# Retention plus MLP on one core: batches 0 and 1 loaded two positions a partition, with 64x64 matmul tiles and a new order of the first stage

## The chip, the core and the metric

The kernel runs on one core of a Trainium2 chip, as one launch. The metric is the device time of one execution in microseconds (us), the median of several runs; lower is better. Besides this, one execution is profiled. Names of engines are those of the profile: PE (matmuls; PEld its weight loads), DVE, ACT and POOL (elementwise work), SP (which issues nearly all DMAs). Each engine works through its own queue in program order.

## The reference

Eight batches of eight heads, 576 positions, head size 64, float32. Attention is without softmax, with a decay for each head; its output goes through a two-layer MLP with a swish whose slope is given for each hidden unit.

```python
def _attn_ref(q, k, v):
    B, H, S, D_ = q.shape                        # 8, 8, 576, 64
    scores = 1.0 / np.sqrt(D_) * np.matmul(q, k.transpose(0, 1, 3, 2))
    gamma = 1.0 - 2.0 ** (-5.0 - np.arange(H, dtype=np.float32))
    rel = np.arange(S)[:, None] - np.arange(S)[None, :]
    Dmat = np.where(rel >= 0, gamma[:, None, None] ** rel[None, :, :], 0.0)
    return np.matmul(scores * Dmat[None], v).astype(np.float32)

def _moe_ref(x, w_in, w_out, beta):              # 4608x512, 512x2048, 2048x512, 2048
    h = x @ w_in
    g = h * (1.0 / (1.0 + np.exp(-beta * h)))
    return (g @ w_out).astype(np.float32)

x = attn_out.transpose(0, 2, 1, 3).reshape(B * S, H * D)     # then _moe_ref
```

## The kernel before

**Attention in chunks.** The decay is split into factors of the query and of the key position: q is multiplied by `gq`, v by `gv`, and the scores get a mask of zeros and ones only. The first 512 positions of a batch are four chunks of 128 (c = 0 to 3); the last 64 positions of all batches are done together at the end. For a chunk the kernel computes scores (keys on the partitions, `a_sc`), masks them with `causal` into `R` (DVE), and adds two matmuls up in one output `O`: values times `R` (`a_O`), and, for c > 0, the state of the earlier chunks times q (`a_cross`). The state is the running sum of keys times values (`a_st`, PSUM tile `st`), copied to `sbds[c]` in bfloat16. `a_x` copies `O` into `xT`, the MLP's input.

**Layouts of batches 0 and 1.** q is loaded with four positions on a partition (`load_q`, 1 KB runs), half of the heads at a time. k and v of a chunk are loaded with one position on a partition (`load_kv`, 256-byte runs, 256 KB each). `pre_q` scales q (DVE), `pre` casts k to `kn` and scales v to `vn` (POOL), `t_q` and `t_k` turn q and k on PE into a PSUM tile `T`, which ACT or DVE copies to `qT` and `kT`. Scores use 64x128 tiles of PE (two heads in the two halves of the rows), outputs 128x64, states and cross terms 128x128. Batches 2 and on have another layout, 64x64 tiles, and turn q and k by DMA; the change leaves them as they are.

**Loads.** SP issues, in this order: q of batch 0 in two halves; k and v of chunks 0 and 1, k of chunks 2 and 3, v of chunks 2 and 3; w_in in eleven pieces; then, in the merged part, w_out, q and k and v of batch 1, q of batch 2, and so on.

**The first stage** (lines 869 to 915) is written out by hand, in program order; `warm_up(n)` are float32 matmuls on zeros between the real ones. Their PSUM tile has the tag `mm`, of which there are three buffers; `O` and `sc` have two each, `st` one.

**The merged part.** `fill` is the list of PE's dense steps (up- and down-projections of the blocks), with `d0` the step of the first down-projection and `u1` the step of the second block's first up-projection. `streams` are lists of (step, function); `merged` puts each function into program order ahead of the step with that number. Batch 1's attention steps and the loads and preparation of the later batches are such streams. From block 3 on, the down-projection is done with seven products in place of eight (`seven_mm`, `seven_a`, `seven_b`).

Of the kernel before, what the change touches and what calls it, by code (L numbers as in the profile page):

```python
# [19 lines left out]
def kernel(  # L20
# [54 lines left out]
    q_tiles, kv_tiles = {}, {}  # L75
# [13 lines left out]
    def load_kv(n, js=(0, 1)):  # L89
# [7 lines left out]
        for j in js:  # L97
            src = (k, v)[j][b].rearrange("h s d -> s h d")
            if b < QB:
                nc.sync.dma_start(t[:, j], src[c * P:(c + 1) * P])  # L100
            elif c % 2 == 0:
                nc.sync.dma_start(t[:, j], src[c * P + TL:(c + 1) * P + TL])
            else:
                for x, at in enumerate(((c - 1) * P, (c + 1) * P - TL)):
                    nc.sync.dma_start(t[x * TL:(x + 1) * TL, j], src[at:at + TL])


    ahead = [(0, 0), (0, 1), (1, 0), (1, 1), (2, 0), (3, 0), (2, 1), (3, 1)]
    keys_first = [(0, 0), (1, 0), (0, 1), (1, 1), (2, 0), (3, 0), (2, 1), (3, 1)]
# [12 lines left out]
    load_q(0)  # L122
    for n, j in ahead:
        load_kv(n, (j,))
# [9 lines left out]
    for j, (step, mul) in enumerate(((1, CB), (P, 1))):  # L134
        nc.gpsimd.iota(pos[:, j, :CB], pattern=[[step, CB]], base=0, channel_multiplier=mul,
# [10 lines left out]
    for h in range(H):  # L146
# [12 lines left out]
    causal = consts.tile([P, P], BF16, name="causal")  # L159
    nc.gpsimd.memset(causal[:], 1.0)  # L160
    nc.gpsimd.affine_select(out=causal[:], in_=causal[:], pattern=[[1, CB], [CB, PC]], compare_op=ALU.is_ge,
                            fill=0.0, base=0, channel_multiplier=-1)
# [38 lines left out]
    def cast_w_in(g, kos=None):  # L201
        t = wts[g]
        f0, fn, rows = pieces[g]
        for ko in kos or range(rows[0].start, rows[-1].stop):
            if ko % 2 == 0:
                nc.gpsimd.tensor_copy(w_in_sb[:, ko, f0:f0 + fn], t[:, ko])  # L206
                continue
            nc.vector.tensor_copy(w_in_sb[:, ko, f0:f0 + fn], t[:, ko])
# [56 lines left out]
    def betas():  # L265
        pb = psum.tile([P, FO], F32, name="pb", tag="mm", bufs=3)
        nc.tensor.transpose(pb[:], beta_rows[:], ident_f[:FO, :FO])
        nc.scalar.copy(beta_sb[:], pb[:])
# [24 lines left out]
    def row_of(b, c):  # L293
        return CB + 1 + c % 2 * 2 + c // 2 if b >= QB else c
# [15 lines left out]
    def pre_q(b, n):  # L310
# [4 lines left out]
        if b < 2:  # L315
            hs, cs = slice(n // 2 * HP, (n // 2 + 1) * HP), slice(n % 2 * 2, n % 2 * 2 + 2)
            e = nc.vector
# [12 lines left out]
    def pre(i, js=(0, 1)):  # L330

        b, c = seq[i]
        if 0 not in js:
            v, g = kv_tiles.pop(i)[:, 1], gains(gv, row_of(b, c))
            if b < QB:
                nc.gpsimd.tensor_tensor(live[i]["vn"][:], v, g, ALU.mult)
            else:
                by_halves(live[i]["vn"], v, g)
# [24 lines left out]
        for to, hs in turned if b >= QB else [(slice(0, H), slice(0, H))]:  # L363
            nc.gpsimd.tensor_copy(kn[:, c % 2, to], t[:, 0, hs])  # L364
        if 1 in js:
            pre(i, (1,))

# [16 lines left out]
    def t_q(b, u):  # L384
        T = psum.tile([P, CB, 2, P], BF16, name="T", tag="mm" if u else "O", bufs=3 if u else 2)
        for i in range(CB):
            for p in range(2):
                nc.tensor.transpose(T[:, i, p, :], heads(batch[b]["qs"][:, i], 2 * u + p), ident[:])
        (nc.vector.tensor_copy if u else nc.scalar.copy)(batch[b]["qT"][:, :, 2 * u:2 * u + 2], T[:])

    def t_k(i):
        T = psum.tile([P, HP, P], BF16, name="T", tag="sc" if i in (CB + 2, CB + 3) else "O", bufs=2)
        for p in range(HP):
            nc.tensor.transpose(T[:, p, :], heads(live[i]["kn"], p), ident[:])
        (nc.vector.tensor_copy if i in (CB + 2, CB + 3) else nc.scalar.copy)(live[i]["kT"], T[:])

# [6 lines left out]
    def a_sc(i):  # L403
        L = live[i]
        L["R"] = R = sb.tile([P, 2, HP, P], BF16, name="R", tag="R", bufs=3)

        tag = "mm" if i == CB - 1 else "O" if i >= E and (i - E) % 2 else "sc"
        sc = [psum.tile([P, HP, P], F32, name="sc", tag=tag, bufs=3 if tag == "mm" else 2) for _ in range(2)]
        for p in range(HP):
            for j in range(2):  # L410
                r = slice(j * D, (j + 1) * D)
                rhs, view = q_cols(i, r, p)
                nc.tensor.matmul(view(sc[j][:, p, :]), L["kT"][r, p, :], rhs, start=True, stop=True,  # L413
                                 skip_group_check=True)
        m_b = causal[:].unsqueeze(1).to_broadcast([P, HP, P])
# [3 lines left out]
    def split(i):  # L419
        return i in (CB - 1, CB + 1)  # L420

    def new_O(i):
        b, c = seq[i]
        if split(i):
            tags = ("sc", "sc") if i == CB - 1 else ("O", "sc")
            live[i]["O"] = [psum.tile([P, 2, P], F32, name="O", tag=t, bufs=2) for t in tags]
# [22 lines left out]
    def a_O(i):  # L449

        b, c = seq[i]
        L = live[i]

        early = i < E
        if not early:
            new_O(i)
        R, vn = L["R"], L["vn"]
        crossed = c > 0
        for j, p in [(n % 2, n // 2) for n in range(H)]:
            nc.tensor.matmul(O_of(i, p)[j * D:(j + 1) * D], vn[:, 2 * p + j, :], R[:, j, p, :],  # L460
                             start=opens(i, p) and not (early and crossed), stop=early or not crossed,
                             skip_group_check=True)

    def a_x(i):
# [3 lines left out]
        if split(i):  # L468
            nc.vector.tensor_copy(x[:, :2], view(Os[0]))
            nc.scalar.copy(x[:, 2:], view(Os[1]))  # L470
# [3 lines left out]
    def a_st(i):  # L474

        b, c = seq[i]
        L = live[i]
        if c == 0:
            state_ps[b] = psum.tile([P, HP, P], F32, name="st", tag="st", bufs=1)
        st = state_ps[b]  # L480
        for p in range(HP):
            nc.tensor.matmul(st[:, p, :], heads(L["kn"], p), heads(L["vn"], p),
                             start=(c == 0 and p == 0), stop=True, skip_group_check=True)
        for j in range(2):
            r, cols = slice(j * D, (j + 1) * D), slice(j * D, (j + 1) * D)
            e = nc.vector.tensor_copy if i in (CB + 2, CB + 3) else nc.scalar.copy
            if c < CB - 1:
                e(sbds[c][r, :, cols], st[r, :, cols])
                continue
            e(ends[b][r, :2], st[r, :2, cols])  # L490
            e(ends[b][(1 - j) * D:(2 - j) * D, 2:], st[r, 2:, cols])
# [377 lines left out]
    warm_up(5)  # L869
    betas()  # L870
    betas_safe()
    for n in range(4):
        pre_q(0, n)
    t_q(0, 0)
    warm_up(1, 128)
    t_q(0, 1)
    pre(0)
    t_k(0)
    warm_up(2, 128)
    a_sc(0)  # L880
    a_st(0)
    pre(1)
    t_k(1)
    warm_up(1, 128)
    a_cross(0, True)
    a_O(0)
    a_x(0)
    a_sc(1)
    a_cross(1, True)
    pre(2, (0,))  # L890
    t_k(2)
    a_st(1)
    a_O(1)
    pre(3, (0,))
    a_sc(2)
    t_k(3)
    a_x(1)
    warm_up(1, 128)
    a_sc(3)
    a_cross(2, True)  # L900
    pre(2, (1,))
    a_st(2)
    a_O(2)
    a_x(2)
    pre(3, (1,))
    warm_up(2, 128)
    a_cross(3, True)
    a_O(3)
    cast_w_in(0, (0, 1))
    a_x(3)  # L910
    cast_w_in(0, (2, 3))
    a_st(3)
# [38 lines left out]
    def second(i):  # L951
        for f in (a_O, lambda j: a_cross(j, False), a_x):
            f(i)
            f(i + 1)
        a_st(i + 1)
# [5 lines left out]
               [(10.3, F(load_q, 1))] + [(10.3, F(load_kv, CB + n, (j,))) for n, j in keys_first],  # L961
# [5 lines left out]
               [(d0 + 8, F(pre, 4, (0,))), (d0 + 8, F(pre, 5, (0,))), (d0 + 9, F(pre, 4, (1,))), (d0 + 9, F(pre, 5, (1,))),  # L967
# [139 lines left out]
```

## Time and profile before

| what | value |
|---|---|
| median of the runs | 293.27 us (three runs, 292.98 to 293.93) |
| the profiled execution | 292.41 us |
| its span, from the first to the last instruction | 290.7 us |
| mean granted clock of PE | 0.999 |
| busy in the span | PE 281.9 (97%), PEld 175.7, DVE 186.1, ACT 171.5, POOL 139.1 us |
| first up-projection matmul (L819) | 18.44 us |
| DMA, 0 to 14.5 us | 216 GB/s |
| DMA, 18.4 to 40 us | 378 GB/s |

PE's matmuls are pipelined, so that its busy share is not a share of its peak; a hole in its row is read from the starts of its matmuls. "Idle before" names the engine or DMA whose work the profile infers to have ended a wait.

### The profile page before, as it was taken

How to read it: one execution, taken by the hardware profiler on the slowest of the kernel's cores; microseconds unless marked ns; L12 is line 12 of the kernel's file. 1: busy time of each engine (PE TensorE's matmuls, PEld its weight loads, DVE VectorE, ACT ScalarE, POOL GpSimd, SP SyncE). 2: the span in 40 equal slices, each digit the busy share in tenths (PEclk: the TensorE clock that was granted, in tenths of full speed). 3: DMA queues.
4: the chain of work that ended last, by engine and by line, in shares of the span. 5: the costliest groups of instructions: out<-in, count | busy, mean ns of one | idle time of the engine just before them, and what ended most of it. 6: DMA issues, size and time to landing. Idle time of an engine off the chain costs nothing.

```text
span 290.7 us, 8297 instructions
## 1 busy us (share of the span) xinstructions
PE 281.9 (97%) x3433; PEld 175.7 (60%) x3433; DVE 186.1 (64%) x340; ACT 171.5 (59%) x301; POOL 139.1 (48%) x259
## 2 busy tenths in 40 slices
PE   8799999999999998999999999999999999999995
PEld 6554446864544554448854885578547845784584
DVE  6563555804896396279889875995597555642673
ACT  5677546686878872765158625772576156837730
POOL 4766207872499397089759539625088100000000
PEclk9999999999999999999999999999999999999999
DMA  8999999996989999988999989990779430003004
GB/s 213 218 342 386 387 283 233 240 190 123 247 180 246 253 187 201 267 225 214 183 249 265 195 231 260 189 156 2 215 176 142 92 144 3 2 28 119 0 4 143
DMA packets 128886, 54.03 MB, mean 186 GB/s; under 512 B 110400, under 2 KB 121680, under 8 KB 128848
## 3 DMA queue, kind: packets, MB, share of 16 engines
q1 hardware_dynamic: 128816, 53.49, 77.9%
q8 instruction: 27, 0.44, 0.7%
q14 instruction: 11, 0.09, 0.1%
q10 hardware_dynamic: 32, 0.01, 0.0%
HBM read 36.71 MB, written 9.44 MB: 159 GB/s over the span
## 4 chain that ended last, share of the span: by engine, by line
PE 55%; DVE 5%; POOL 4%; DMA 2%; issue 1%; ACT 0%; SPq 0%; DVEq 0%
PE ph L727 27%; PE U L764 10%; PE Z L764 7%; PE W L764 6%; DMA qn<-in_q_dram 2%; DVE sa L748 2%; PE O L509 2%; PE po L837 2%; POOL vn L305 2%; POOL kn L364 1%; PE sc L509 1%; POOL qs L323 1%; PE st L509 1%; DVE gT L732 1%; DVE R L286 1%
## 5 line engine op out<-in xcount | busy, mean ns | idle before, releaser
L727 PE MATMUL ph<-xT,w_in_sb 128*128 128x512 bf16 (+1 forms) x560 | 116.8, 364 | 0.0
L727 PEld LDWEIGHTS <-w_in_sb 128*128 128x128 bf16 x560 | 53.3, 98 | 55.2 <-POOL w_in_sb L206 0.7
L734 ACT ACTIVATE gT<-ph,beta_sb 128x512 bf16<-128x512 f32 (+1 forms) x92 | 58.4, 642 | 42.6 <-PE ph L727 41.8
L764 PEld LDWEIGHTS <-sa 128*128 128x128 bf16 x480 | 46.9, 98 | 5.8 <-issue 0.2
L732 DVE TENSOR_SCALAR gT<-hs,ratio 128x512 bf16<-128x512 f32 x48 | 25.8, 538 | 32.9 <-ACT hs L731 32.6
L364 POOL CAST kn<-kvn 128x128 bf16<-128x128 f32 (+2 forms) x80 | 35.8, 483 | 22.3 <-DMA kvn<-in_k_dram 21.8
L323 POOL TENSOR_TENSOR qs<-qn,gq 128x256 bf16<-128x256 f32 x48 | 30.5, 667 | 33.2 <-DMA qn<-in_q_dram 23.4
L748 DVE TENSOR_TENSOR sa<-gT 128x1024 bf16<-128x1024 bf16 (+1 forms) x54 | 43.9, 854 | 1.4 <-PE Z L764 1.2
L731 ACT ACTIVATE hs<-ph,beta_sb 128x512 f32<-128x512 f32 x48 | 33.0, 688 | 19.0 <-PE ph L727 18.7
L837 PE MATMUL po<-w_out_sb,gT 128*128 128x512 bf16 x192 | 43.5, 379 | 0.0
L305 POOL TENSOR_TENSOR vn<-kvn,gv 128x256 bf16<-128x256 f32 x48 | 34.3, 739 | 1.2 <-DMA kvn<-in_v_dram 0.7
L837 PEld LDWEIGHTS <-gT 128*128 128x128 bf16 x192 | 18.1, 98 | 20.6
L764 PE MATMUL U<-b,sa 128*128 128x256 bf16 x192 | 22.9, 272 | 0.1
L764 PE MATMUL Z<-b,sa 128*128 128x256 bf16 x192 | 22.9, 273 | 0.0
L286 DVE TENSOR_TENSOR R<-sc,late 128x512 bf16<-128x512 f32 x24 | 15.4, 681 | 11.4 <-issue 10.2
L764 PEld LDWEIGHTS <-gT 128*128 128x128 bf16 x192 | 18.7, 98 | 3.5
L248 DVE TENSOR_TENSOR b<-wt 128x512 bf16<-128x512 f32 x20 | 16.4, 880 | 1.9 <-ACT wt L231 1.8
L417 DVE TENSOR_TENSOR R<-sc,causal 128x512 bf16<-128x512 f32 x16 | 10.2, 686 | 4.6 <-PE sc L413 4.5
L819 PE MATMUL ph<-xT,w_in_sb 128*128 128x512 bf16 x56 | 12.4, 379 | 0.2 <-ACT xT L470 0.2
L642 ACT CAST xT<-O 128x512 bf16<-128x512 f32 x19 | 9.8, 599 | 3.5 <-PE O L509 3.5
L764 PE MATMUL W<-b,gT 128*128 128x256 bf16 x96 | 11.5, 273 | 0.0
L764 PE MATMUL U<-b,gT 128*128 128x256 bf16 x96 | 11.5, 273 | 0.0
(118 smaller groups left out, 304.8 us busy)
## 6 DMA issues: line engine op xcount, KB each, us to landing
qn<-in_q_dram SPq DMA_DIRECT2D x16, 512.0 KB, 5.8
out_dram<-ot SPq DMA_DIRECT2D x32, 256.0 KB, 3.3
kvn<-in_k_dram SPq DMA_DIRECT2D x20, 256.0 KB, 5.4
kvn<-in_v_dram SPq DMA_DIRECT2D x20, 256.0 KB, 5.1
wt<-in_moe_w_out_dram SPq DMA_DIRECT2D x8, 512.0 KB, 9.3
kvn<-in_k_dram SPq DMA_DIRECT2D x24, 128.0 KB, 4.0
kvn<-in_v_dram SPq DMA_DIRECT2D x24, 128.0 KB, 3.4
wt<-in_moe_w_in_dram SPq DMA_DIRECT2D x5, 512.0 KB, 8.2
```

The lines of the kernel that those rows point to most:

```text
L248: nc.vector.tensor_tensor(to, x, y, op)
L286: return lambda: f(*a)
L305: nc.gpsimd.tensor_tensor(vn[:, hs], v[:, hs], g[:, hs], ALU.mult)
L323: nc.gpsimd.tensor_tensor(batch[b]["qs"][:, cs, to], q_tiles[b][:, hs, cs].rearrange("p h i d -> p i h d"), gq[:, cs, hs].unsqueeze(3).to_ ...
L364: nc.gpsimd.tensor_copy(kn[:, c % 2, to], t[:, 0, hs])
L727: nc.tensor.matmul(ph, w_in_sb[:, ko, fo * P:(fo + 1) * P], xts[m][:, ko, :, w], start=(ko == 0), stop=(ko == KO - 1))
L731: nc.scalar.activation(h, ph, ACT.Silu, scale=beta_sb[:, fo:fo + 1])
L732: nc.vector.tensor_scalar(gts[m][:, fo], h, ratio[:, fo // 2:fo // 2 + 1], None, ALU.mult)
L734: nc.scalar.activation(gts[m][:, fo, :, w], ph, ACT.Silu, scale=beta_sb[:, fo:fo + 1])
L748: nc.vector.tensor_tensor(sums_a[0][:, held_in[j], ks], quarter(m, *x, ks), quarter(m, *y, ks), op)
L764: nc.tensor.matmul(chains[c, n][:, 0 if alone else p], a, sevens[k // 2][:, j - 1, k % 2, :], start=j in (3, 4, 1) and k == 0 and (alone o ...
L837: nc.tensor.matmul(po[:, :nn], gT[:, fo, ms, :], w_out_sb[:, fo, n0:n0 + nn], start=(fo == 0), stop=(fo == FO - 1))
```

## The change

k and v of batches 0 and 1 are loaded 256 positions at a time, two neighbouring positions on a partition (`load_span`, 512 KB in 512-byte runs). Partition p of span u holds positions 256u + 2p + r, r = 0, 1; so one half of the partitions (`half(x)`) holds chunk 2u + x. Scores, outputs and states are therefore done on 64 rows, with two matmuls (r = 0, 1) where there was one; scores and outputs go in two steps of four heads (`y`), both chunks of the span together, with 64x64 tiles. The states of chunks 0 and 1 are made in one step (`states(b, 0)`: the first from one half of the partitions, the second from all 128). `causal` and `pos` follow the layout. Masks, transposes, copies and casts are as many elements as before.

The first stage is ordered anew. SP: q of heads 0 to 3, k of span 0, q of heads 4 to 7, v of span 0, k and v of span 1. The beta row is turned ahead of most warm-ups, and its copy goes from ACT to DVE. One of four steps of batch 0's q goes from DVE to POOL, one of the four key casts from POOL to DVE, and the casts of w_in's first piece go to POOL alone. Chunk 2's outputs are split in two PSUM tiles, as chunk 3's were. In the merged part batch 1's steps stand at the places of the old ones.

```diff
-            if b < QB:
-                nc.sync.dma_start(t[:, j], src[c * P:(c + 1) * P])
...
+    def load_span(b, u, j):
+        t = stage.tile([P, H, 2, D], F32, name="kvn", tag="kvn", bufs=NQ)
+        nc.sync.dma_start(t[:].rearrange("p h r d -> p h (r d)"),
+                          (k, v)[j][b][:, 2 * u * P:2 * (u + 1) * P].rearrange("h (p r) d -> p h (r d)", r=2))
+        span_tiles[b, u, j] = t
...
-    load_q(0)
-    for n, j in ahead:
-        load_kv(n, (j,))
+    load_q(0, (0,))
+    load_span(0, 0, 0)
+    load_q(0, (1,))
+    load_span(0, 0, 1)
+    load_span(0, 1, 0)
+    load_span(0, 1, 1)
...
+    def t_k(b, u, r):
+        late_span = b and u
+        T = psum.tile([P, HP, P], BF16, name="T", tag="sc" if late_span else "O" if b or u + r == 0 else "mm", ...)
...
+        (nc.vector.tensor_copy if late_span or u > r else nc.scalar.copy)(spans[b, u]["kT"][:, r], T[:])
...
+    def a_sc(b, u, y):
+        L["R"][y] = R = sb.tile([P, 2, 2, 2, P], BF16, name="R", tag="R", bufs=3)
+        tag = ("O" if b else "mm") if y else "sc"
+        sc = [psum.tile([P, 2, 2, P], F32, name="sc", tag=tag, bufs=3 if tag == "mm" else 2) for _ in range(2)]
+        def one(j, r, pp, x):
+            rhs, view = q_cols(b * CB + 2 * u + x, row_d(j), 2 * y + pp)
+            mm(view(sc[j][half(x), r, pp, :]), L["kT"][row_d(j), r, 2 * y + pp, half(x)], rhs, start=True)
+        paired(*[[F(one, j, r, pp, x ^ j) for r in range(2) for pp in range(2) for x in range(2)] for j in range(2)])
...
+    def a_O(b, u, y, crossed=(), last=True):
+        def one(x, pp, r, hh):
+            i, p = b * CB + 2 * u + x, 2 * y + pp
+            mm(O_of(i, p)[row_d(hh)], L["vn"][r][half(x), 2 * p + hh, :], L["R"][y][half(x), hh, r, pp, :],
+               start=opens(i, p) and r == 0 and x not in crossed, stop=last and r == 1)
...
+    def states(b, c):
+        for n, rows in ((0, half(0)), (1, slice(0, P))) if c == 0 else ((1, half(c % 2)),):
+            for r in range(2):
+                for p in range(HP):
+                    for j in range(2):
+                        mm(st[row_d(j), n, p, :], L["kn"][rows, r, 2 * p + j, :], L["vn"][r][rows, 2 * p + j, :], ...)
...
+    warm_up(1)
     betas()
     betas_safe()
-    for n in range(4):
+    warm_up(3)
+    for n in range(2):
         pre_q(0, n)
     t_q(0, 0)
+    for r in range(2):
+        pre_k(0, 0, r)
+        warm_up(1, 128)
+        t_k(0, 0, r)
+    for n in range(2, 4):
+        pre_q(0, n)
     warm_up(1, 128)
+    a_sc(0, 0, 0)
+    t_q(0, 1, (slice(0, 2), slice(2, CB)))
+    for r in range(2):
+        pre_v(0, 0, r)
     warm_up(2, 128)
+    a_sc(0, 0, 1)
+    warm_up(2, 128)
+    states(0, 0)
+    state_out(0, 0)
+    pre_k(0, 1, 0, nc.vector.tensor_copy)
+    pre_k(0, 1, 1)
+    for c in range(2):
+        new_O(c)
+    a_O(0, 0, 0)
+    for r in range(2):
+        t_k(0, 1, r)
+    a_O(0, 0, 1, last=False)
+    a_cross(1, False)
+    state_out(0, 1)
+    for r in range(2):
+        pre_v(0, 1, r)
     a_x(0)
+    a_sc(0, 1, 0)
     a_x(1)
+    a_sc(0, 1, 1)
+    warm_up(2, 128)
     a_cross(2, True)
+    new_O(3)
+    warm_up(2, 128)
+    states(0, 2)
+    state_out(0, 2)
+    a_O(0, 1, 0, (0,))
+    cast_w_in(0, (0, 1), True)
+    cast_w_in(0, (2, 3), True)
+    a_O(0, 1, 1, (0,))
+    a_cross(3, False)
     a_x(2)
     a_x(3)
+    states(0, 3)
+    state_out(0, 3)
...
     def second(i):
-        for f in (a_O, lambda j: a_cross(j, False), a_x):
+        for f in (new_O, lambda j: a_O(1, j % CB // 2, j % 2, last=False), lambda j: a_cross(j, False), a_x):
             f(i)
             f(i + 1)
-        a_st(i + 1)
+        if i == CB:
+            state_out(1, 1)
+        else:
+            states(1, 3)
+            state_out(1, 3)
...
-               [(10.3, F(load_q, 1))] + [(10.3, F(load_kv, CB + n, (j,))) for n, j in keys_first],
+               [(10.3, F(load_q, 1))] + [(10.3, F(load_span, 1, u, j)) for u in range(2) for j in range(2)],
...
+               [(d0 + 8, F(pre_k, 1, 0, r)) for r in range(2)] + [(d0 + 9, F(pre_v, 1, 0, r)) for r in range(2)] +
+               [(d0 + 12.7, F(t_k, 1, 0, 0)), (d0 + 13.4, F(t_k, 1, 0, 1)), (d0 + 14, F(a_sc, 1, 0, 0)), (d0 + 15, F(a_sc, 1, 0, 1)),
+                (d0 + 15, F(states, 1, 0)), (d0 + 15, F(state_out, 1, 0)), (d0 + 15.9, F(second, 4))],
```

167 lines of the change are left out of this document (57 added, 110 removed).

## The prediction

> **What bounds the kernel now.** I read the page's slices first, then the windows by stage, the timeline of the first 19 us, PE's timeline around its one long hole, and SP's waits. Slices (tenths; GB/s is what the DMA engines moved):
>
> ```profile
> PE   8799999999999998999999999999999999999995
> GB/s 213 218 342 386 387 283 233 240 190 123 247 180 246 253 187 201 267 225 214 183 249 265 195 231 260 189 156 2 215 176 142 92 144 3 2 28 119 0 4 143
> ```
>
> PE is full but for the first slices; the loads run at 213 and 218 GB/s there and at 386 soon after. The windows (PE, PEld, DVE, ACT, POOL busy, then clock, DMA share, GB/s):
>
> ```profile
> 18.40:40.00 21.60, 21.56 (x100) 9.60 (x101) 9.93 (x26) 12.98 (x23) 7.98 (x16) 1.00 1.06 378
> 40.00:56.00 16.00, 16.00 (x183) 10.44 (x181) 10.67 (x19) 9.86 (x21) 9.65 (x13) 1.00 1.10 237
> ```
>
> From 18.4 us PE has no hole up to 56. So what counts is when the first up-projection (L819) starts, what PE work batch 1 needs, and any hole later. The timeline of the first stage (start, length, what; in brackets the idle time and who ended it):
>
> ```profile
> 4.76 1.29 DVE L326 TENSOR_TENSOR qs<-qn,gq 128x512 bf16<-128x512 f32 x2 [0.46 <-DMA qn<-in_q_dram]
> 6.23 1.31 DVE L326 TENSOR_TENSOR qs<-qn,gq 128x512 bf16<-128x512 f32 x2 [0.17 <-DMA qn<-in_q_dram]
> ...
> 13.47 0.62 POOL L364 CAST kn<-kvn 128x512 bf16<-128x512 f32 x1 [0.60 <-DMA kvn<-in_k_dram]
> 14.70 2.19 POOL L336 TENSOR_TENSOR vn<-kvn,gv 128x512 bf16<-128x512 f32 x2 [0.60 <-DMA kvn<-in_v_dram]
> 16.40 0.75 ACT L488 CAST sbd<-st 64x256 bf16<-64x256 f32 x2 [0.56 <-PE st L482]
> 17.20 0.40 PE L446 MATMUL O<-qT,sbd 128*128 128x128 bf16 x4
> 17.87 0.42 DVE L469 CAST xT<-O 128x256 bf16<-128x256 f32 x1 [0.49 <-PE O L460]
> 18.44 5.34 PE L819 MATMUL ph<-xT,w_in_sb 128*128 128x512 bf16 x24 [0.17 <-ACT xT L470]
> ...
> 25.80 0.43 DVE L208 CAST w_in_sb<-wt 128x512 bf16<-128x512 f32 x1 [0.93 <-DMA wt<-in_moe_w_in_dram]
> 27.16 0.43 DVE L208 CAST w_in_sb<-wt 128x512 bf16<-128x512 f32 x1 [0.93 <-DMA wt<-in_moe_w_in_dram]
> ```
>
> The last loads of v (14.7, and 15.8 by the second of the pair at 14.70) release the last state (16.4 to 17.15), the cross term (17.20), the last output and xT (18.3). The arrival rate sets this stage: 256 KB in 256-byte runs each 1.2 us (13.47 to 14.70), 512 KB of q in 1 KB runs 1.47 us, 512 KB of w_in in 2 KB runs 1.36 us. PE's timeline where its one long hole is:
>
> ```profile
> 107.92 0.71 PE L509 MATMUL O<-R,vn 64*64 64x64 bf16 x64
> 110.03 0.19 PE L509 MATMUL st<-vn,kn 64*64 64x64 bf16 x1 [1.03 <-POOL vn L305]
> 110.61 0.38 PE L509 MATMUL st<-vn,kn 64*64 64x64 bf16 x24 [0.32 <-POOL vn L305]
> ...
> 111.20 1.04 PE L837 MATMUL po<-w_out_sb,gT 128*128 128x512 bf16 x4
> ```
>
> From 107.92 to the next dense matmul at 111.20 are 3.28 us; the same block in the chain runs from 160.06 to 161.84, 1.78. The hole is worth 1.5 us.
>
> **The change, part by part.** *Loads.* A 512 KB load in 512-byte runs lies between 1.4 us (the 2 KB row) and 2.4 us (two 256-byte loads). Per run and per one of 16 DMA engines the rows give 19 ns at 256 bytes, 46 at 1 KB; on that line 512 bytes take 28 ns, so 64 runs take 1.8 us. I take 1.8. Four such loads save 4 x 0.6 = 2.4 us of the 9.6 that k and v take in each of batches 0 and 1, so w_in, w_out and batch 1's q come 2.4 us earlier, and batch 2's q over 3 us earlier (it gains again behind batch 1). [...]
>
> *First stage.* But earlier data help only if the engines keep up, so I list the new order with durations of the trace and 0.05 us from one engine to the next (the same list for the order of before ends at 18.5, against 18.44). q of heads 0-3 lands at 4.7, k of the first 256 positions at 6.5, the other q at 8.0, then v 9.8, k 11.6, v 13.4. POOL is free for k at 6.4: the two mask selects (nearest rows 0.32 and 0.28, twice) end by 4.8, the beta steps, now from a DVE copy, take 1.6; anything over the 0.1 left there costs one to one. POOL casts two halves of k (0.61 each): 7.7. PE turns them (0.40), ACT copies them one after the other (0.59): 8.8. Scores of heads 0-3: 9.25 (16 matmuls on four tiles; the rows are 8 in 0.40 at L413 and 32 half as wide in 0.45 at L509, so 0.3 to 0.5; I take 0.40). The q transposes of heads 4-7 stand behind those scores: 9.8. q on POOL (two 128x256 at 0.6 by L323, 8.06 to 9.26) hides under that. ACT copies both parts (0.59 each): 10.85. Scores of heads 4-7: 11.3. Two masks on DVE (0.69, the second 0.61 later): 12.6. Only then comes DVE's cast of half of the next span's k (0.43; its data lay there since 11.6): 13.0. Transposes, a copy on DVE and one on ACT (0.59): 14.3. Scores: 14.75. Four masks, 0.61 apart: third done 16.7, last 17.3. The second warm-up ahead of states(0, 2) takes the third "mm" buffer after the scores whose mask is the third, if the three go round in order of request; no row shows that. So it waits until 16.75, and the states behind it on PE's queue start at 17.3, though v was scaled at 15.55: 0.45, then two state copies on ACT (0.37 each): 18.6. Cross 0.40: 19.0; xT 0.42: 19.5. First up-projection 19.55: **1.05 us later** than the list of before. The four w_in casts, all on POOL now (0.40 each from 15.55), end at 17.2 under this. If that buffer doesn't hold the states, the last mask does: 17.3, output, cross, xT, and L819 at 18.75, +0.25. Between 1.4 and 2.4 us a load, L819 moves from 19.4 to 20.7.
>
> *Batch 1 beside dense matmuls.* PE's queue is what counts. Scores, outputs and transposes take the same PE time (half as big, twice as many, four at once). States become 64 small matmuls, at about 15 ns by the L509 row (32 in 0.45, with the last one's 0.19 to drain) for 16 at 55 ns: 0 to +0.3, I take 0.05. Between shapes PE pauses:
>
> ```profile
> 66.81 1.03 PE L837 MATMUL po<-w_out_sb,gT 128*128 128x512 bf16 x4
> 67.76 0.45 PE L509 MATMUL sc<-qT,kT 64*64 64x64 bf16 x32
> ```
>
> Four dense matmuls at 0.216 would be past at 67.67; the small ones start at 67.76: 0.09. Counting shape changes along the streams: 12 before, 17 after (states in two shapes, the last states behind the crosses): +5 x 0.09 = 0.45. **+0.5 us** in all. Data come earlier, so I book no new wait; masks, copies and casts are as many as before.
>
> *The hole at 109.* It ends when POOL has batch 4's v. That work hangs on a chain of loads and POOL steps that starts with batch 2's q:
>
> ```profile
> 52.82 1.19 POOL L323 TENSOR_TENSOR qs<-qn,gq 128x256 bf16<-128x256 f32 x2 [0.35 <-PE sc L413]
> 54.39 3.49 POOL L323 TENSOR_TENSOR qs<-qn,gq 128x256 bf16<-128x256 f32 x6 [0.38 <-DMA qn<-in_q_dram]
> ```
>
> The first names scores, but those are issued later in the program (step u1+3 against d0+12.5), so it can't wait for them; I take the load, as in the second. SP's waits between 50 and 112 us (in total, times, longest) name POOL, hardly anything else:
>
> ```profile
> SPq L372 <- POOL vn L305: 8.4, 7, 2.2
> SPq L372 <- POOL kn L364: 3.7, 2, 1.9
> SPq L86 <- DVE sum L545: 0.4, 1, 0.4
> ```
>
> So this chain moves with the loads, 2 to 3 us earlier, while PE comes 1.5 later: **-1.5 us**, the hole closes. PE's short waits for w_in casts (PEld 0.40 at 23.69, overlapped) go too, -0.1.
>
> **Sum.** 1.05 + 0.5 - 1.5 - 0.1 = -0.05. The profiled execution took 292.41 us (span 290.7 and 1.7 around it), the median of the runs is 293.27, 0.86 more; so 292.4 in a profile and **293.2** in the median: no change.
>
> **Rivals.** (a) Faster: the warm-up does not hold the states; L819 at 18.75, and with loads near 1.5 us another 0.1 to 0.2 off: sum -0.95, 292.3. For: the buffer order is only read from the code. Against: each request of a three-buffer tag should take the oldest. (b) Slower: the hole at 109 moves along with PE, because the POOL chain starts with something PE releases. The rows at 52.82 (scores) speak for it, program order and SP's waits against. Then -1.5 is missing: +1.45, 294.7; it decides as soon as v of batch 4 is over 0.9 us later than now. (c) Slower: 512-byte runs do no better per byte than 256 (which is also the case that the change doesn't do what it says): L819 at 20.7, sum +1.1, 294.3; it decides from about 2.3 us a load. (d) Slower: PE's clock. The warm-up matmuls of the start take 0.46 us for 256 columns up to 5.9 us, later ones about 0.12 for 128, half of it per column; the up-projections of before start at full speed (24 in 5.34). The new order has fewer warm-ups at the start and PE waits up to 0.9 us at a time near 16. Were PE slow again at 19.5 for as long as at the start, about 4 us, it would cost 2 us: 295.2. [...]
>
> **How the numbers follow.** Forecast 0.37, (a) 0.31, (b) 0.20, (c) 0.07, (d) 0.05. About 0.3% (0.9 us) is what a measurement of this kernel tells from no change. So faster 0.31, same 0.37, slower 0.32. The range takes in (a) with a little over for batch 1, and (b) and (c) up to a shortfall of 2 us: 291.7 to 295.2; (d) and worse lie outside. The forecast's own range is 292.4 to 294.
>
> **What would show it.** Right: the second k cast's POOL row at 7.1, v of the last span landing near 13.4; DVE's four masks back to back from 14.8; warm-ups of L262 idle before states(0, 2) until the third mask; L819 at 19.5; w_in casts without DMA waits; batch 2's first qs row near 49.5; no POOL wait of PE at 109 to 111. Wrong: k landing after 7, L819 before 19 or after 20, or the hole at 109 still there.

## The result and the profile after

The changed kernel takes 294.12 us (median of 20 runs) beside 293.0 us for the kernel before in the same rounds; the ratio is 1.005, 95% interval 1.0031 to 1.0069. By the ratio it is slower by about 1.5 us, where no change was forecast; the medians differ by 1.1 only, since the ratio leaves out the slow executions (one of the changed kernel, 483.28 us at a granted clock of 0.562, and three of the kernel before, above 297 us). A second measurement of the same kernel, beside other runs, gave 1.0064 (1.0043 to 1.0086). The profiled execution took 294.08 us with a span of 292.4 us: 1.7 us more than before.

The two traces were laid beside each other at the starts of the same PE work:

| place | before, us | changed, us | late by |
|---|---|---|---|
| first up-projection | 18.44 | 19.04 | 0.60 |
| scores of batch 2 | 67.76 | 69.87 | 2.11 |
| outputs ahead of the hole at 109 | 107.92 | 110.89 | 2.97 |
| scores behind it | 122.53 | 123.72 | 1.19 |
| end of the span | 290.7 | 292.4 | 1.7 |

So the first stage cost 0.6, batch 1 cost 1.5, something near 104 cost 0.9, the hole at 109 gave back 1.8, and 0.5 was lost later, at 171.

The windows by stage of the changed kernel (PE, PEld, DVE, ACT, POOL busy with counts, clock, DMA share, GB/s):

```profile
18.40:40.00 21.60, 21.49 (x116) 10.00 (x118) 11.70 (x29) 13.43 (x25) 6.61 (x14) 1.00 1.07 372
40.00:56.00 16.00, 15.01 (x233) 9.53 (x235) 8.38 (x15) 8.76 (x18) 13.17 (x24) 1.00 1.02 254
```

Between 40 and 56 us, where batch 1's work lies, PE was full before (16.00 of 16.00); now 0.99 is missing. Of this, 0.62 are two waits told below (0.44 for kT, 0.18 for xT); the rest is mostly the time of two matmuls whose records are missing (233 beside 235 weight loads). The first stage in the timeline of the changed kernel (start, length, what; in brackets the idle time before it and who ended it):

```profile
13.63 2.05 POOL L384 TENSOR_TENSOR vn<-kvn,gv 128x512 bf16<-128x512 f32 x2 [0.92 <-DMA kvn<-in_v_dram]
15.12 2.48 DVE L438 TENSOR_TENSOR R<-sc,causal 128x512 bf16<-128x512 f32 x4 [0.83 <-PE sc L529]
16.21 0.66 PE L269 MATMUL ph<-warm 128*128 128x128 f32 x4
16.81 0.38 PE L529 MATMUL st<-vn,kn 64*64 64x64 bf16 x12
17.83 0.53 PE L529 MATMUL O<-R,vn 64*64 64x128 bf16 x24 [0.47 <-issue]
19.04 0.81 PE L839 MATMUL ph<-xT,w_in_sb 128*128 128x512 bf16 x2
```

v of the last span lands at 13.6, and the four masks run back to back from 15.12, near the 13.4 and 14.8 of the list. But the second warm-up starts at 16.21 and the states at 16.81, with no wait for the third mask, which ends near 17. What holds the first up-projection is the fourth mask (17.60) and a stop of PE. Eight of the 32 outputs are done when PE stands still, from 17.36 to 17.83; it waits for nothing that the profile names ("issue"), and goes on 0.2 us behind the end of that mask.

The rest of that timeline, at the places that matter:

```profile
46.38 0.31 PE L529 MATMUL sc<-qT,kT 64*64 64x128 bf16 x8
47.12 0.31 PE L529 MATMUL sc<-qT,kT 64*64 64x128 bf16 x8 [0.44 <-ACT kT L416]
...
49.16 2.91 POOL L330 TENSOR_TENSOR qs<-qn,gq 128x256 bf16<-128x256 f32 x5
...
69.87 0.45 PE L529 MATMUL sc<-qT,kT 64*64 64x64 bf16 x32
...
103.42 0.39 PE L529 MATMUL st<-vn,kn 64*64 64x64 bf16 x25
104.56 0.25 PE L529 MATMUL st<-vn,kn 64*64 64x64 bf16 x7 [0.76 <-issue]
...
110.89 0.71 PE L529 MATMUL O<-R,vn 64*64 64x64 bf16 x64
112.62 0.59 PE L857 MATMUL po<-w_out_sb,gT 128*128 128x512 bf16 x2 [0.16 <-issue]
...
164.78 5.80 DVE L768 TENSOR_TENSOR sa<-gT 128x1024 bf16<-128x1024 bf16 x6
164.85 8.33 POOL L330 TENSOR_TENSOR qs<-qn,gq 128x256 bf16<-128x256 f32 x8 [1.85 <-issue]
171.23 1.03 PE L784 MATMUL U<-b,sa 128*128 128x256 bf16 x8 [0.43 <-DVE ot L798]
```

Four things are to be seen. At 47.12 the second half of batch 1's scores waits for a copy of kT that was made in the same block of small matmuls. At 103.4 PE stops in the middle of 32 equal matmuls, 25 before and 7 behind the stop, and the profile names nothing that ends it (0.76 us, "issue"). At 110.89 the 120 outputs and 32 states of the long hole of before run through: 1.50 us to the weight load of the next dense matmul at 112.39, against 3.28 before (the record of that matmul is missing, so the row at 112.62 starts with the one behind it). At 164.8 POOL scales q beside DVE's six additions; these take 0.97 us each, 0.69 before (six in 4.11, with POOL busy 0.56 us of that time), and PE waits for `ot`, the output block into which DVE adds PE's products. The same places in the timeline of the kernel before, where the scores of one chunk ran in one piece:

```profile
45.87 0.40 PE L413 MATMUL sc<-qT,kT 64*128 64x128 bf16 x8
...
164.22 4.11 DVE L748 TENSOR_TENSOR sa<-gT 128x1024 bf16<-128x1024 bf16 x6
```

### The profile page after: what moved, and what is told of

Read it like the earlier page. It is cut to its first block, busy times and chain, and to the rows that moved or that the text cites. A ratio compares the mean times of both kernels' runs of the same rounds, so it can differ in the third digit from the quotient of the medians.

```text
span 292.4 us, 8723 instructions
## 1 busy us (share of the span) xinstructions
PE 281.0 (96%) x3634; PEld 177.7 (61%) x3663; DVE 180.8 (62%) x341; ACT 170.5 (58%) x300; POOL 132.3 (45%) x262
## 4 chain that ended last, share of the span: by engine, by line
PE 84%; DMA 6%; SPq 4%; DVE 2%; issue 2%; ACT 1%; POOL 0%
PE ph L747 38%; PE po L857 14%; PE U L784 10%; PE Z L784 7%; PE W L784 6%; PE O L529 4%; DMA wt<-in_moe_w_out_dram 3%; DMA wt<-in_moe_w_in_dram 3%; PE sc L529 2%; SPq L109 2%; PE st L529 2%; DVE sa L768 2%; SPq L205 1%; PE ph L839 1%; SPq L86 0%
## 5 line engine op out<-in xcount | busy, mean ns | idle before, releaser
L747 PE MATMUL ph<-xT,w_in_sb 128*128 128x512 bf16 (+1 forms) x542 | 114.2, 363 | 1.6 <-issue 0.6
L752 DVE TENSOR_SCALAR gT<-hs,ratio 128x512 bf16<-128x512 f32 x48 | 25.2, 527 | 34.6 <-ACT hs L751 34.1
L330 POOL TENSOR_TENSOR qs<-qn,gq 128x256 bf16<-128x256 f32 x48 | 32.1, 701 | 26.5 <-DMA qn<-in_q_dram 20.1
L857 PE MATMUL po<-w_out_sb,gT 128*128 128x512 bf16 x183 | 42.0, 379 | 1.1 <-issue 1.0
L312 POOL TENSOR_TENSOR vn<-kvn,gv 128x256 bf16<-128x256 f32 x48 | 30.7, 661 | 12.1 <-issue 6.5
L367 POOL CAST kn<-kvn 128x128 bf16<-128x128 f32 (+1 forms) x72 | 24.1, 372 | 17.7 <-DMA kvn<-in_k_dram 17.7
L255 DVE TENSOR_TENSOR b<-wt 128x512 bf16<-128x512 f32 x20 | 13.1, 714 | 3.1 <-ACT wt L238 1.8
L784 PE MATMUL W<-b,sa 128*128 128x256 bf16 x96 | 11.5, 273 | 0.0
```

Of the source, the lines that this page charges most:

```text
L312: nc.gpsimd.tensor_tensor(vn[:, hs], v[:, hs], g[:, hs], ALU.mult)
L330: nc.gpsimd.tensor_tensor(batch[b]["qs"][:, cs, to], q_tiles[b][:, hs, cs].rearrange("p h i d -> p i h d"), gq[:, cs, hs].unsqueeze(3).to_ ...
L747: nc.tensor.matmul(ph, w_in_sb[:, ko, fo * P:(fo + 1) * P], xts[m][:, ko, :, w], start=(ko == 0), stop=(ko == KO - 1))
L752: nc.vector.tensor_scalar(gts[m][:, fo], h, ratio[:, fo // 2:fo // 2 + 1], None, ALU.mult)
L784: nc.tensor.matmul(chains[c, n][:, 0 if alone else p], a, sevens[k // 2][:, j - 1, k % 2, :], start=j in (3, 4, 1) and k == 0 and (alone o ...
L857: nc.tensor.matmul(po[:, :nn], gT[:, fo, ms, :], w_out_sb[:, fo, n0:n0 + nn], start=(fo == 0), stop=(fo == FO - 1))
```

## The experiments

All ratios are to the kernel before, measured in the same rounds; the kernel before itself stood between 291.97 and 293.0 us from one group of rounds to the next, so ratios are compared, not medians. Each edit is to the changed kernel unless the text says otherwise.

**The wait for kT.**

```diff
-(d0 + 12.7, F(t_k, 1, 0, 0)), (d0 + 13.4, F(t_k, 1, 0, 1)),
+(d0 + 11.7, F(t_k, 1, 0, 0)), (d0 + 12.7, F(t_k, 1, 0, 1)),
```

> The changed kernel with the transposes of the two halves of batch 1's first k span one block of small matmuls earlier each (d0 + 11.7 and d0 + 12.7 instead of 12.7 and 13.4); only PE's order changes. Theory W: the wait of 0.6 us at 46.5 is a chain inside one block of small matmuls (transposes, ACT's copy of 0.59, then scores of the same block), which the old order did not have, since scores needed one tile of 128 positions only; with a block of dense matmuls between them it goes: 0.6 us less, 293.5 (the stall at 103.6 may move a little, since 8 instructions change place). Rival: the wait only changes its name (scores then wait for qT, or the masks come later): 294.1.

Ratio 1.0040 (1.0012 to 1.0067), 293.21 us. PE's timeline has the 16 scores in one piece:

```profile
46.57 0.42 PE L529 MATMUL sc<-qT,kT 64*64 64x128 bf16 x16
```

From the first up-projection to the down-projections behind batch 2's scores PE needs 53.30 us, 53.93 in the changed kernel and 52.41 before (starts of the same weight loads). So 0.6 of the 1.5 is this wait, shown at its place. The total hardly shows it: 0.1 us of span in the profiled execution, and by the ratios 0.3, with intervals that overlap. PE lost the gain again at 167, where it now waited 0.7 us for one of DVE's additions.

**The additions beside POOL.** The load of the last batch's q goes behind its k and v:

```diff
-            st += [(at - 30, F(load_q, b))] + ...
+            st += [(at - (25.9 if b == B - 1 else 30), F(load_q, b))] + ...
```

> The changed kernel with the loads of the last batch's q put behind the four k loads and v loads that follow them on SP's queue (time due at - 25.9 instead of at - 30, for that batch only); no other engine's order changes. Theory P: from 164.8 us on POOL scales the last batch's q beside DVE's six additions of 1024 columns, which then take 0.97 us each instead of 0.69 (and POOL's own steps 1.04 instead of 0.62), and so PE waits 0.4 us for ot at 171; before the change POOL came to that work at 170.4, behind the additions. With q later the additions take 0.69 again and the wait goes: 0.4 us less, 293.7. Rival: the additions are slow for another reason (ACT, PE or the DMA queues): still near 0.97, 294.1. A q that comes too late would show as a wait of PE or SP behind 176 us.

Ratio 1.0045 (1.0022 to 1.0068), 293.62 us. DVE's and POOL's timeline:

```profile
165.91 3.69 DVE L768 TENSOR_TENSOR sa<-gT 128x1024 bf16<-128x1024 bf16 x6
170.53 5.74 POOL L330 TENSOR_TENSOR qs<-qn,gq 128x256 bf16<-128x256 f32 x8 [6.53 <-issue]
```

The additions take 0.62 us each, POOL's steps 0.72 instead of 1.04, and PE has no wait behind 150 us. Theory P holds at its place, for some 0.5 us. The total does not show it (span 292.5 us): in this execution the first up-projection stood 0.59 later, and PE stood still for 0.28 near 137. Side by side both engines were slower: 0.97 against 0.62 on DVE, 1.04 against 0.72 on POOL. Why, no run shows.

**The stop at 103.6.** Small matmuls without use at the start, to shift PE's program (the version with 56 has `warm_up(2)` for `warm_up(3)`):

```diff
         pre_q(0, n)
+    pad = psum.tile([P, MB], F32, name="pad", tag="mm", bufs=3)
+    for n in range(20):                                  # or 56
+        mm(pad[row_d(n % 2), :D], ident[row_d(0), row_d(0)], ident[row_d(0), row_d(0)], start=True)
     t_q(0, 0)
```

> The changed kernel with 20 small matmuls (64x64, result unused) added on PE at the start, in the idle time before the first transposes; nothing else moves. Their use is to shift the rest of PE's program by 40 instructions. Theory C (code): the stall of 0.9 us in the middle of 32 states matmuls at 103.6, which ends by no semaphore, is PE waiting for the next 16 KB of its program (256 instructions; the DMA record of the instruction queue starts at 101.70, and PE had run 264 instructions in the 3.9 us before it stopped). Then the boundary falls 40 instructions earlier, the 256 before it take 7 us instead of 3.9, and the stall at 103.6 is gone: 0.9 us less, 293.2, unless another burst takes it. Rival M: PE waits there for another engine by a semaphore that the profile does not name: the stall stays, 0.9 us at the same matmul, and the time stays at 294.1.

> The same with 56 small matmuls, and one of the three warm-up matmuls ahead of them left out so that the start does not get longer: the rest of PE's program is shifted by about 108 instructions. Theory C: the stall at 103.6 is gone here too; by counting 256-instruction blocks on from it, blocks would then lie inside the long runs of small matmuls near 165, 190 and 247 us, where 256 instructions take 1 to 3 us, so new stalls of 1 to 3 us each that end by no semaphore can appear there: 294 to 299. Rival M: the stall at 103.6 stays, nothing new at 165, 190 or 247: 294.1.

20: ratio 1.0105 (1.006 to 1.015). 56: 1.0202 (1.0146 to 1.0258). PE has no wait between 100 and 110 us in either. With 20 the stall came to the first stage instead (states(0, 2), 1.0 us) and the first up-projection stood at 20.05. With 56 the waits of PE between 160 and 200 us are (in total, times, longest):

```profile
PE W L784 <- issue: 2.0, 1, 2.0
PE O L529 <- issue: 0.9, 1, 0.9
```

These are at 167.4, between two dense matmuls of one product, and at 195.3, both foretold; the one near 247 did not come. Two more things made this version slow in the profiled execution, the slowest of its four: the first up-projection stood at 21.0, and behind the stall at 167 the granted clock was 0.50 from 170.0 to 173.4. The same 20 matmuls in the kernel before:

> The kernel before, with the same 20 small matmuls on PE at the start (result unused) and nothing else changed: PE's program is shifted by 40 instructions. Theory C (in all traces so far the stalls that end by no semaphore stand at the same counts of PE instructions, 452 and a multiple of about 256.8 on from it, whatever the kernel, and end 1.4 to 1.6 us behind the end of a 16 KB load of the instruction queue): the kernel before has no such stall only because no block boundary falls badly. Shifted by 40, blocks lie inside the runs of small matmuls near 189 and 246 us, and stalls of 1 to 3 us appear there: 294.5 to 298, for a change that does nothing. Rival: the small matmuls hide at the start and cost nothing: within 0.3 of the kernel before.

Ratio 1.0117 (1.0077 to 1.0156): a change that does nothing costs 3.3 us (295.38 against 292.09). The profiled execution, the slowest of four, took 4.3 us of span more: 0.8 of it is the start (the first up-projection at 19.2: that much did not hide), 2.2 the foretold stall at 191, and two waits of 0.7 for DVE at 141 and 154 are most of the rest; no stall came near 246. The stall in the wait list:

```profile
PE O L509 <- issue: 2.2, 1, 2.2
```

Counting PE's weight loads from the start of the span to the middle of each stall (the windows view) gives 223 in the first stage, whether 20 matmuls were put ahead of it or six or four warm-up matmuls taken away; 1244 at 104 in the changed kernel, in q_last and in two_edits; 1755 at 136 to 137 (q_last, two_edits); 2265 and 2647 with 56 small matmuls; 2391 in the kernel before with 20. From 223 these are 8.0, 12.0, 16.0, 18.9 and 16.9 times 128. A weight load and a matmul are two instructions (the page counts them apart, 3433 each in the kernel before), so these stalls stand multiples of 256 instructions of PE's program apart, to within 16, whatever the work there. The instruction queue agrees: its q8 moved 27 records of 16 KB (0.44 MB) in the kernel before and 28 (0.46 MB) in the changed one, beside 6866 and 7326 weight loads and matmuls, which is 254 and 262 a record. The stalls ended 1.4 to 2.1 us behind the end of such a record; in the changed kernel the records end at 16.44 and 102.97, and PE goes on at 17.83 and 104.56. So I read them as waits for the next part of PE's program ("stalls for code"): an inference from the counts, the shifts and the records. How much of its program PE holds, no run shows. At 103.6 the 256 had run in 3.8 us (two bursts of small matmuls close together).

The size of a stall differs between executions, and so does the start of the record ahead of it (101.70 in the first trace of the changed kernel, 100.62 in the second): at count 1244 PE stood from start to start 0.95, 0.95, 1.15 and 0.30 us (changed, q_last, two_edits, tk_early), and not at all in the second trace of the changed kernel:

> The changed kernel once more, beside the run above on the same chip, for its own ratio and a second trace. If the readings of the first trace hold: 0.6 us at PE's scores for kT near 46.5, 0.7 to 0.95 at the states near 103.6 with no releaser, 0.4 to 0.6 at 170.5 for ot, no wait for POOL's v near 109; ratio 1.004 to 1.006. If the stall near 103.6 were a chance of one execution, it would be missing here.

Ratio 1.0064 (1.0043 to 1.0086). The wait for kT, the missing hole and a smaller wait for ot (0.2) were there, the stall at 103.6 was not, and that execution's span was 291.5, 0.9 less than the first. So the place is fixed and the size is chance; my expectation left no room for that.

**The loads.** Each span's load as two DMAs of 256-byte runs:

```diff
-        nc.sync.dma_start(t[:].rearrange("p h r d -> p h (r d)"), ... "h (p r) d -> p h (r d)" ...)
+        for r in range(2):
+            nc.sync.dma_start(t[:, :, r], ... "h (p r) d -> p h r d" ...[:, :, r])
```

> The changed kernel with each of the eight loads of k and v of batches 0 and 1 made as two DMAs, one for the even and one for the odd positions, so that every run is 256 bytes again; tiles, engines' orders and all else as in the changed kernel. Theory L (the loads move the chain behind the hole at 109): 512 KB then take 2.4 us instead of 1.77, v of the last span lands 2.5 us later and the first up-projection starts 0.6 to 1.6 us later; batch 2's first scaled q comes 3 to 5 us later, POOL's work on batch 4's v with it, and the hole of 1 to 1.5 us at 109 is back, while the slow additions at 165 to 171 get faster again: 295.5 to 297. Rival N (the new order of PE and POOL closed the hole): the hole stays closed, only the first stage is later: 294.7 to 295.5. Rival D: two DMAs of 256-byte runs take no longer than one of 512-byte runs: 294.1.

Ratio 1.0085 (1.0054 to 1.0117), 294.65 us. Timeline of PE and POOL:

```profile
19.91 1.45 PE L839 MATMUL ph<-xT,w_in_sb 128*128 128x512 bf16 x6
...
53.46 1.19 POOL L330 TENSOR_TENSOR qs<-qn,gq 128x256 bf16<-128x256 f32 x2 [1.18 <-PE T L415]
...
105.90 1.18 POOL L312 TENSOR_TENSOR vn<-kvn,gv 128x256 bf16<-128x256 f32 x2 [0.62 <-DMA kvn<-in_v_dram]
```

The first up-projection is 0.87 later than in the profiled execution of the changed kernel. The eight traces with the changed kernel's first stage have it between 18.9 and 19.6, since the stall in that stage differs too; so the longer runs are worth 0.3 to 1.0 us there (theory L for this stage). But PE has no wait at 109, though batch 2's first q is scaled at 53.46, later than before the change (52.82): POOL's v for batch 4 starts at 105.90, 108.94 before and 102.22 in the changed kernel. Theory L fell for the hole; it closes without the earlier loads. What gives POOL those 3 us between 53 and 106 was not isolated.

**The warm-up matmuls.** The six ahead of states(0, 0), a_cross(2) and states(0, 2) are left out (three times `-    warm_up(2, 128)`).

> The changed kernel without the six warm-up matmuls ahead of states(0, 0), of the cross term of chunk 2 and of states(0, 2) (24 PE instructions less ahead of everything that follows). Theory C: block boundaries fall 24 instructions later in the program, the stall at 103.6 shrinks from 0.9 to 0.2 us or less and the one in the last outputs of batch 0 (17.4 to 17.8, 0.2 us behind the last mask) goes: the first up-projection 0.2 us earlier, in all 0.9 us less, 293.2, unless a new boundary hurts near 138 or 163. The forecast on record had these warm-ups hold states(0, 2) until the third mask; the trace of the changed kernel shows the states starting before that mask ends, so without them states(0, 2) start near 15.8 instead of 16.8, and the first up-projection still waits for the fourth mask: at most 0.25 us earlier. Rival: PE's clock drops without them and small matmuls and up-projections behind 16 us get slower, by 0.5 us or more.

Ratio 1.0131 (1.0096 to 1.0166), 295.96 us: the rival. Windows (PE busy first, the clock in the third column from the end):

```profile
16.00:20.00 4.00, 2.60 (x73) 1.87 (x73) 2.88 (x7) 2.48 (x7) 2.59 (x8) 1.00 1.09 361
20.00:24.00 4.00, 4.00 (x12) 1.44 (x11) 2.70 (x10) 1.96 (x6) 2.50 (x4) 0.57 1.05 386
```

All four executions show a lower granted clock (0.986 to 0.994). The up-projections of 512 columns run at 0.43 us, 0.216 otherwise, up to 23.5 us, and from the first to the 61st weight load of the up-projections PE needs 14.5 us against 12.8: 1.7 lost. In the four microseconds before, PE was busy 2.60 (3.47 in the changed kernel) and never idle for longer than 0.7. The states began at 16.82 all the same, held by the cross term's wait for a copy, and the first up-projection stood at 19.8. So the half clock (0.57 granted in the mean from 20 to 24 us) came behind less work and short idles. What brings it on, this run does not show.

**Edits together.** First the two that held and the six warm-ups:

> The changed kernel with three edits together: the transposes of batch 1's first k span one block earlier, the last batch's q loaded behind its k and v, and the six warm-up matmuls left out. If the three terms are independent: 0.6 (wait for kT) + 0.4 to 0.5 (additions beside POOL) + 0.9 (two stalls for code) less than the changed kernel's 294.1, so 292.1 to 292.3, about 0.7 to 0.9 below the kernel before. Rival: PE, earlier by 1.5 us, runs into the next wait (POOL's v near 109, or batch 2's q), or a block boundary of the code falls badly: 293 or more.

Ratio 1.0078 (1.0042 to 1.0114). The profiled execution (296.70 us) is the slowest of eight. Its first up-projection stood at 21.4, and the half clock came again (0.43 us a matmul from 21.4 to 26.0), for 2.3 us, which hides the rest. Six of the eight show a granted clock of 0.988 to 0.994; the other two took 293.02 and 293.77 us. Then the two alone, and the two with `warm_up(2, 128)` as `warm_up(1, 256)` in four places:

> The changed kernel with the two edits that held alone, together: the transposes of batch 1's first k span one block earlier, and the last batch's q loaded behind its k and v. All warm-up matmuls stay. Theory: the terms add: 0.6 (wait for kT) + 0.5 to 0.6 (additions beside POOL), and some 0.5 of the stall for code at 103.6, which had shrunk to 0.3 in the first of the two alone: 1.5 below the changed kernel, about the kernel before: ratio 0.998 to 1.001. Rival: PE, earlier, waits elsewhere (in the first edit alone, PE waited 0.9 for an addition at 167, since POOL's scaling fell on the additions more squarely), and the ratio stays near 1.003.

> The same two edits, and each of the four pairs of warm-up matmuls of 128 columns made one of 256 columns: the same PE time, but 16 PE instructions fewer ahead of the rest (a matmul in fp32 is four instructions here). Theory C: the blocks of 256 instructions move 16 instructions later in the program, so what is left of the stall at 103.6 goes (0.3), and the stall near 136 moves into dense matmuls: 0.3 to 0.6 less than with the two edits alone, ratio 0.996 to 0.999. PE's clock stays up, as the warm-up time is the same: the first up-projections at 0.216 us per 512 columns, against 0.43 without warm-ups. Rival: a boundary falls worse elsewhere (138 or 163 by the count): no gain or a loss of up to 0.5.

Two edits: 1.0043 (1.0022 to 1.0064), span 291.4, 1.0 less than the changed kernel's; the wait for kT and the slow additions are gone, the stalls for code were 1.15 (103) and 0.75 (136) from start to start. Shifted: 1.0061 (1.0037 to 1.0085). The stalls at 103 and 136 are gone, but the one in the first stage grew:

```profile
18.91 0.42 PE L529 MATMUL O<-R,vn 64*64 64x128 bf16 x16 [1.82 <-issue]
```

and behind that gap the up-projections run at 0.43 us again. That is the slowest of twelve executions (295.11 us). Ten of them show a granted clock of 0.998 or more, so the half clock does not explain their median, and the ratio is not to be told from that of the two edits alone. At last the shift was put behind the first stage, with batch 1's first 16 scores issued twice:

> The two edits, with all warm-up matmuls as in the changed kernel, and the 16 score matmuls of batch 1's first span and heads 0 to 3 issued twice in a row (same result): 32 PE instructions more, placed behind the first stage, so that the first stage keeps its code blocks and its clock. Theory C: blocks move 32 instructions earlier in the program from 46 us on; the stalls at 103 (0.9 beyond a small gap) and 135.6 (0.5) of the two edits go, the 16 matmuls cost 0.25 on PE, and a stall of up to 0.3 may come near 152, as with the 20 small matmuls at the start: 0.9 to 1.1 less than the two edits alone, a span near 290.4, ratio 1.000 to 1.002. Rival: the stalls at 103 and 135 stay (they belong to the work there, not to the count of instructions): a span of 291.6, ratio 1.004 to 1.006.

Ratio 1.0043 (1.0019 to 1.0066), span 291.4. Both stalls are gone, as theory C has it, and PE's last work comes 0.55 earlier; but the first stage's stall was larger in this execution (the first up-projection 0.45 later) and the last stores took 0.6 longer to end. No gain in the total.

**Batch 1 undone.** `load_kv`, `t_k`, `a_sc`, `a_O`, `a_st` and the steps of the kernel before for batch 1; batch 0 as changed:

```diff
-[(10.3, F(load_span, 1, u, j)) for u in range(2) for j in range(2)]
+[(10.3, F(load_kv, CB + n, (j,))) for n, j in keys_first]
...
-(d0 + 14, F(a_sc, 1, 0, 0)), (d0 + 15, F(a_sc, 1, 0, 1)), (d0 + 15, F(states, 1, 0)), ...
+(d0 + 14, F(a_sc1, 4)), (d0 + 15, F(a_sc1, 5)), (d0 + 15, F(a_st1, 4)), ...
```

> Only batch 0 in the new layout: batch 1's loads (256-byte runs), scores, outputs, states and their steps are those of the kernel before; its v gains come from four more columns of the table and its mask from a tile made at d0 + 6. Theory H: of the 2.1 us by which PE is late at batch 2's scores, 0.6 comes from batch 0's stage and 1.5 from batch 1's blocks; so the first up-projection starts near 19.1 as in the changed kernel, but batch 2's scores stand at 68.0 to 68.3 (67.45 before, 69.56 changed). POOL's chain keeps most of its lead, so the hole of 1.8 at 109 stays closed or nearly so; the additions at 165 to 171 collide with POOL as in the changed kernel (0.4 to 0.6); with 224 PE instructions fewer the code blocks fall as in the kernel with 32 more, so no stall at 103 or 135. Span 290.7 + 0.6 - 1.6 + 0.5 = 290.2, ratio 0.997 to 1.000. Rival: batch 1 is not what costs (PE late by 2 us at batch 2 all the same), or the chain of POOL loses its lead with batch 1's loads and the hole at 109 is back: 1.002 or more.

> The same, with the last batch's q loaded behind its k and v as before: theory P of the additions says 0.4 to 0.6 less than the one above, span 289.7, ratio 0.995 to 0.998: faster than both kernels. Rival: as above, or q comes too late: no gain.

Ratios 0.9986 (0.9962 to 1.0010) and 1.0001 (0.9972 to 1.0030). PE's timeline of the first:

```profile
68.36 0.45 PE L597 MATMUL sc<-qT,kT 64*64 64x64 bf16 x32
...
110.54 2.75 PE L925 MATMUL po<-w_out_sb,gT 128*128 128x512 bf16 x12 [0.16 <-issue]
```

Batch 2's scores are 0.60 late (68.36 against 67.76; the expectation's figures for this place are 0.31 lower in both kernels), about the first stage's share in this execution (0.69); the other 1.5 was batch 1. At 110.54 PE is ahead of the kernel before (111.20) and has no wait for POOL, though it came to the outputs ahead of the hole only 0.64 late (108.56): POOL's v for batch 4 started at 103.48. So POOL's lead closes the hole by itself. By the ratio this is 1.9 to 2.3 us below the changed kernel (1.0050 or 1.0064 against 0.9986), and not to be told from the kernel before: PE was 0.6 late ahead of the hole and 0.9 early behind it, 0.9 went into a stall for code and a wait for DVE near 150 us, and the last stores ended 0.85 later behind PE's last matmul. The collision that I expected to stay at 165 to 171 was not there (the six additions took 3.69 us, and POOL scaled the last q from 169.99 on, behind them), and so moving the last q brought nothing more. No version beat the kernel before measurably.

## Why the prediction was right or wrong, step by step

The sum forecast 1.05 + 0.5 - 1.5 - 0.1 = -0.05; the two profiled executions differ by 0.6 + 1.5 + 0.9 - 1.8 + 0.5 = 1.7 (0.8 in the second trace of the changed kernel, which lacks the 0.9). Three failed steps made the forecast too fast: batch 1's term was 1.0 too small, and the stall for code (0.9) and the additions beside POOL (0.5) stood at nothing. Two made it too slow: the first stage and the hole came out 0.7 better together. That the median still came within 0.9 us of the forecast is luck: the errors had opposite signs.

*Loads: right.* The four loads of k and v took 1.74 to 1.83 us each, from one landing to the next, and k landed at 6.64; forecast 1.8 and 6.5. The same bytes of w_in in 2 KB runs took 1.36. Rival (a) took off another 0.1 to 0.2 for loads near 1.5 us; no run shows a load of 512-byte runs that short.

*First stage, 1.05: over-sized, measured 0.60.* The chain came as listed up to the four masks. The step that failed is the warm-up that was to hold states(0, 2) through its buffer. It did not; the text's own alternative, that the last mask decides (18.75), came within 0.3. The 0.60 holds for one execution: the eight traces with this first stage give 0.5 to 1.2, with a stop of up to 0.9 in its last outputs. The short waits for w_in casts, -0.1, went as forecast: PE's lateness falls from 0.58 to 0.51 between 18 and 26 us.

*Batch 1 beside dense matmuls, 0.5: this term failed, measured 1.5.* The shape changes were sized well: a block of states alone takes 0.37 us from its first matmul to the next dense one, 0.22 before, close to what 0.09 a change and 0.05 give. What failed is "I book no new wait". In the new layout the scores of a span need both halves of kT; the second half is turned, copied by ACT (0.59) and used inside one block of small matmuls: 0.6. A further 0.2 is PE's wait for xT at 51.6. The rest, some 0.2, stays unassigned.

*The hole at 109, -1.5: size right, reason only partly.* It closed and gave 1.78. POOL's chain did move earlier (q at 49.16, as forecast, and v of batch 4 at 102.22 instead of 108.94), and with batch 1 undone its lead closed the hole with PE only 0.64 late. But that lead does not come from the loads alone, since the hole closes also where batch 2's q comes later than before. In the changed kernel PE came 3 us later to a place where it would have waited 1.8 anyway, so its lateness alone would have closed the hole too: it came to these states at 111.7, and even before the change v was there at 110.6.

*Left out of the sum.* The stall for code, 0 to 1.15 us in one execution, 0.9 in the profiled one: some 460 PE instructions more (3663 weight loads with their matmuls against 3433), in bursts of small matmuls. And the other side of POOL's lead, 0.5: the text said that the chain comes earlier, and did not ask what POOL's work would then run beside.

*Rivals.* (b) gives nearly the time that came, but for a reason that did not occur: the hole did not move with PE. (c) was wrong. (d) did not occur in this kernel, but is real: with six warm-ups less it cost 1.7 us; its chance of 0.05 rested on no run. The granted clock showed it: 0.57 in a window of 4 us.

## What to carry to other kernels

When a chain off the critical path comes earlier, ask both what it releases and what it will run beside; here the same lead, together with PE's lateness, closed a hole of 1.8 us, and took 0.5. When work is cut into smaller matmuls, look for a copy that now lies between two steps of one block on an in-order queue (here a wait of 0.44 us for kT), and count instructions: here PE stood still for 0.95 us behind 256 instructions run in 3.8 us, and even an idle edit, 20 unused matmuls, moved the stalls and cost the kernel before 1.2%. To judge an edit of 0.3%, look at its place in the trace, since the total carries all of these.

## What the runs showed of the hardware

PE's stalls for code stood multiples of 256 instructions apart, to within 16, and lasted up to 2.2 us; 20 unused matmuls cost the kernel before 1.2%. PE's clock fell to half with PE busy 65% of the 4 us before and no gap over 0.7 us (fewer_warm), or behind one gap of 1.8 us (two_shifted) or 2.0 us (pad56), and cost 1.3 us (pad56) to 2.3 us (all_three). A gap of 0.9 us in the first stage (two_padded) did not do it, nor did one of 2.2 us at 191 (before_pad20, granted clock 1.00 behind it). So the length of a gap does not decide it alone; what does was not isolated.
